# Merging two residue tails per key tile in a dilated attention and soft MoE kernel

The kernel runs on one core of one Trainium2 chip. The metric is the device time of one launch in microseconds (us). The profile of one execution gives its span, which is about 1.7 us shorter than that time. An execution that is clearly longer than the fastest of the same kernel (by over 1.5%) is called slow, and only fast ones are compared.

## The reference

Attention over 8 batches of 8 heads, 576 positions, head size 64. Four heads see the last 32 positions. The other four see every fourth of the last 128, so each of their positions meets only keys of its own residue modulo 4. A soft mixture of experts follows on the 4608 rows of 512.

```python
rel = pos[:, None] - pos[None, :]
mask_plain = (rel >= 0) & (rel < 32)
mask_dil = (rel >= 0) & (rel < 128) & (rel % 4 == 0)
scores = np.where(masks, 0.125 * np.matmul(q, k.transpose(0, 1, 3, 2)), -1e9)
x = softmax(scores) @ v                 # (4608, 512) after the heads are joined
logits = x @ phi                        # 32 slots, 4 for each of 8 experts
d = softmax over the 4608 rows of logits
slot_out[e] = relu((d.T @ x)[e] @ w1[e]) @ w2[e]
out = softmax over the 32 slots of logits @ slot_out
```

## The kernel before

A residue has 144 positions (`SUB`): one tile of 128 and a tail of 16 (`LEFT`). The results of the four tails of a head share one block of 128 rows in `xd`, 32 rows for each, of which 16 are wanted. After the change they fill 64 rows (`NLEFT`). A loop over the batches emits, on TensorE, masks and scores, then products with the values, transposes of the results, logits and slot sums.

```python
def emit_scores(b, g):                    # stage g == 1 holds the tails
    ...
        for r in range(DIL):
            w = LEFT if r < 3 else 2 * LEFT
            jobs.append((kd, SUB * r + 96, qd, SUB * r + 128, W1 + LEFT * r, w))
    ...
    for h in range(4):                    # the mask comes in as a product with ident
        nc.tensor.matmul(sps[h // 2][:, h % 2, 0:n], ident, bias[g], start=True, ...)
    for jn, (kt_, k0, qt_, q0, c0, w) in enumerate(jobs):
        for tt in range(2):
            for h in range(4):
                nc.tensor.matmul(..., kt_[32 * h : 32 * h + 32, k0 : k0 + 128, tt],
                                 qt_[32 * h : 32 * h + 32, q0 : q0 + w, tt], ...)

def emit_av(b, kind, i):                  # a chunk of 6 or 7 (tile, head) units
    ...
        elif t < DIL:                     # whole dilated tiles: 128 rows of output
            jobs.append((0, 128, n, pt[:, h % 2, 128 * t : 128 * t + 128], vD[...]))
        else:                             # tails: four products of 32 rows of output
            for r in range(DIL):
                c0 = W1 + LEFT * r
                jobs.append((32 * r, 32, n, pt[0:48, h % 2, c0 : c0 + 32],
                             vL[b % NV][0:48, h, r, 0 : D + 1]))
    jobs += over                          # overhangs of the plain heads, 32 rows of output
    for k, (p0, np_, n, l, rr) in enumerate(jobs):
        nc.tensor.matmul(o[p0 : p0 + np_, n, :], l, rr, ...)

def back_xT_dil(b, c):
    for r in range(DIL + 1):
        nc.tensor.transpose(rg[:, 128 * r : 128 * r + 128],
                            xd_t[b][:, r, 128 * c : 128 * c + 128], ident)

def slot_out(half, experts):              # products of 256 columns
    for e in experts:
        for c in range(8):
            nc.tensor.matmul(so[half][32 * a : 32 * a + 32, :], hTm[...],
                             w2t[e][:, c, NH * half : NH * half + NH], ...)
```

In `emit_av` the second number of a job is the width of the piece of the array's output that one product uses: 128, or 32.

The softmax here doesn't subtract the row's maximum and nothing guards it: scores larger than these inputs give would overflow.

## Time and profile before

| | before |
|---|---|
| median of 6 runs, us | 182.07 (181.59 to 182.62) |
| profiled span, us | 181.0 |
| TensorE (PE) busy, share of the span | 81% |
| one batch of the loop at full clock, us | 13.67 (101.49 to 115.16) |
| first store issued, us | 152.88 |

The batch is measured between the same product of two successive batches, in a stretch where the granted clock was full.

First the slices of the granted TensorE clock (40 equal slices of the span, 9 is 90% or more of full speed):

```profile
PEclk9999995798589789789999999999855699879855
```

Four lines of the timeline (start, length, engine, line, operation, shapes, count). Lengths of successive products overlap and their ends are modelled, so costs are read from start to start:

```profile
103.08 0.47 PE L339 MATMUL o_d<-v,p 128*128 128x65 f16 x18
103.48 0.53 PE L377 MATMUL rp<-ident,xp 128*128 128x128 f16 x5
...
106.45 0.73 PE L389 MATMUL rd<-ident,xd 128*128 128x128 f16 x10
107.02 0.38 PE L271 MATMUL sa<-masks,ident 128*128 128x512 f16 x1
```

The 18 value products of the chunk with the tails take 103.48 - 103.08 = 0.40 us. The last update of the slot sums shows when the loop ends, and the view of waits shows how long the engine that issues the stores stood before the first one:

```profile
136.80 0.32 DVE L458 TENSOR_TENSOR UT<-UT,u 128x160 f32<-128x160 f32 x1 [1.15 <-PE u L452]
```

```profile
POOL out_dram L746 <- DVE oo L743: 5.8, 1, 5.8
```

### The profile page before, as it was taken

The page shows a single profiled execution, that of the slowest core. Times are in us where ns is not written, and L with a number is a line of the kernel's source. Part 1 is how long each engine was busy: PE and PEld are TensorE (multiplying, and loading weights), DVE is VectorE, ACT ScalarE, POOL GpSimd, SP SyncE. Part 2 cuts the span into 40 slices and gives each one's busy share as a digit, 9 for nine tenths or more (in the row PEclk, how much of TensorE's full clock was granted, in tenths as well). Part 3 has the DMA queues.
Part 4 walks back from the last instruction along what each step waited for, and adds up shares of the span by engine and source line. Part 5 has one row for each costly group of instructions (what it writes and reads, how often), then busy time and mean ns, then how long its engine had stood idle before and what let it go on. Part 6 is the DMA issues. An engine that isn't in the chain of part 4 may idle for free.

```text
span 181.0 us, 5591 instructions
## 1 busy us (share of the span) xinstructions
PE 146.4 (81%) x2464; PEld 87.4 (48%) x2464; DVE 107.5 (59%) x232; ACT 91.0 (50%) x162; POOL 83.9 (46%) x124
## 2 busy tenths in 40 slices
PE   0467977999999999999999999999987986598000
PEld 0133544746755665664674674675735363233000
DVE  4689874875757676588498498453604023389030
ACT  2044454748465484755766776675430024488030
POOL 7953552642623263352544327434410442979900
PEclk9999995798589789789999999999855699879855
DMA  4999999999999999999999999999999999999996
GB/s 60 199 196 208 208 210 214 201 211 214 202 212 214 203 212 214 201 211 213 203 214 211 204 216 210 214 215 215 211 216 213 200 193 163 311 332 409 410 404 239
DMA packets 29527, 40.75 MB, mean 225 GB/s; under 512 B 1856, under 2 KB 19264, under 8 KB 29504
## 3 DMA queue, kind: packets, MB, share of 16 engines
q0 software_dynamic: 28960, 39.36, 116.3%
q1 hardware_dynamic: 544, 1.05, 1.5%
q8 instruction: 19, 0.31, 0.6%
q14 instruction: 4, 0.03, 0.0%
HBM read 61.93 MB, written 9.44 MB: 394 GB/s over the span
## 4 chain that ended last, share of the span: by engine, by line
DMA 43%; PE 34%; ACT 6%; DVE 6%; POOL 5%; issue 3%; POOLq 0%; DVEq 0%
DMA w<-in_moe_w_dram 28%; DMA raw<-in_k_dram 9%; ACT p L293 5%; PE lg L408 5%; PE o_p L339 4%; PE sa L282 4%; DMA out_dram<-ol 4%; PE sb L271 4%; PE sa L271 4%; DMA out_dram<-ot 2%; PE rd L389 2%; DVE qk L245 2%; PE vb L163 2%; PE va L163 2%; PE u L452 2%
## 5 line engine op out<-in xcount | busy, mean ns | idle before, releaser
L293 ACT ACTIVATE p<-sa 128x960 f16<-128x960 f32 (+2 forms) x24 | 21.4, 891 | 33.9 <-PE sb L282 33.4
L339 PEld LDWEIGHTS <-p 128*128 128x128 f16 (+2 forms) x544 | 19.7, 99 | 12.8 <-issue 8.6
L245 DVE STREAM_TRANSPOSE qk<-raw 128x320 uint32<-128x320 uint32 (+1 forms) x32 | 21.6, 678 | 0.3
L271 PE MATMUL sa<-masks,ident 128*128 128x480 f16 (+2 forms) x48 | 15.6, 414 | 7.3 <-POOL masks L489 6.2
L293 ACT ACTIVATE p<-sb 128x960 f16<-128x960 f32 (+2 forms) x24 | 21.2, 884 | 0.0
L236 DVE STREAM_TRANSPOSE qk<-raw 128x576 uint32<-128x576 uint32 x16 | 19.8, 1249 | 0.9 <-DMA raw<-in_q_dram 0.8
L271 PEld LDWEIGHTS <-ident 128*128 128x128 f16 x96 | 9.6, 112 | 18.9 <-issue 7.7
L282 PEld LDWEIGHTS <-qk 32*128 32x128 f16 x832 | 12.6, 100 | 12.0 <-issue 9.8
L408 PE MATMUL lg<-xTd,phi 128*128 128x288 f16 x32 | 18.3, 659 | 0.0
L339 PE MATMUL o_p<-v,p 128*128 128x65 f16 (+1 forms) x288 | 16.6, 202 | 0.8 <-ACT v L172 0.7
L282 PE MATMUL sa<-qk 32*128 32x160 f16 (+4 forms) x416 | 16.5, 217 | 0.8 <-DVE qk L236 0.7
L282 PE MATMUL sb<-qk 32*128 32x160 f16 (+4 forms) x416 | 16.5, 218 | 0.0
L271 PE MATMUL sb<-masks,ident 128*128 128x480 f16 (+2 forms) x48 | 15.4, 411 | 0.5 <-ACT p L293 0.5
L209 POOL COPY v<-v 32x1024 f16<-32x1024 f16 x8 | 8.3, 1036 | 16.1 <-PE sb L282 9.4
L212 POOL DMA_DIRECT2D w<-in_moe_w_dram x16 | 8.9, 554 | 14.4 <-DMA vs<-in_v_dram 6.8
L361 DVE TENSOR_TENSOR xp<-o_p,rc_p 128x448 f16<-128x448 f32 (+1 forms) x24 | 14.4, 602 | 0.8
L361 DVE TENSOR_TENSOR xd<-o_d,rc_d 128x448 f16<-128x448 f32 (+1 forms) x24 | 14.4, 602 | 0.8
L219 POOL DMA_DIRECT2D w<-in_moe_w_dram x10 | 6.7, 673 | 14.5 <-DMA w<-in_moe_w_dram 10.2
L163 PE MATMUL va<-vs,orders 32*128 32x256 f16 (+1 forms) x96 | 12.1, 289 | 1.0 <-ACT p L293 1.0
L412 ACT ACTIVATE ET<-lg 128x288 f16<-128x288 f32 x16 | 6.6, 411 | 12.3 <-PE lg L408 12.1
L360 DVE RECIPROCAL rc_p<-o_p 128x7 f32<-128x7 f32 (+1 forms) x24 | 4.8, 198 | 12.1 <-PE o_p L339 11.6
L382 ACT COPY xTp<-rp 128x576 f16<-128x576 f16 x16 | 10.4, 647 | 2.2 <-PE rp L377 2.2
(108 smaller groups left out, 277.9 us busy)
## 6 DMA issues: line engine op xcount, KB each, us to landing
w<-in_moe_w_dram POOLq DMA_DIRECT2D x16, 512.0 KB, 16.8
w<-in_moe_w_dram POOLq DMA_DIRECT2D x5, 1024.0 KB, 19.3
vs<-in_v_dram POOLq DMA_DIRECT2D x8, 512.0 KB, 14.5
raw<-in_q_dram POOLq DMA_DIRECT2D x7, 576.0 KB, 16.6
raw<-in_k_dram POOLq DMA_DIRECT2D x7, 576.0 KB, 16.8
out_dram<-ot POOLq DMA_DIRECT2D x14, 256.0 KB, 4.2
out_dram<-of POOLq DMA_DIRECT2D x7, 512.0 KB, 4.9
w<-in_moe_w_dram POOLq DMA_DIRECT2D x8, 256.0 KB, 10.2
```

Of the source, the lines that this page charges most:

```text
L163: nc.tensor.matmul(o.rearrange("p (h d) -> p h d", h=4), l, st[:, 0:4, D * r : D * r + D], start=(r == 0), stop=(r == DIL - 1), skip_group ...
L209: nc.gpsimd.tensor_copy(out=vL[b % NV][0:32, :, :, 0:D], in_=vD[b % NV][96:128, :, :, 0:D])
L212: nc.gpsimd.dma_start(out=w1t[e][:, 2 * i : 2 * i + 2, :].rearrange("p l f -> p (l f)"), in_=moe_w1[e, 256 * i : 256 * i + 256].rearrange( ...
L236: nc.vector.transpose(out=dst, in_=src)
L245: nc.vector.transpose(out=o, in_=i)
L271: nc.tensor.matmul(sps[h // 2][:, h % 2, 0:n], ident, bias[g], start=True, stop=False, skip_group_check=True,)
L282: nc.tensor.matmul(sps[h // 2][:, h % 2, c0 : c0 + w], kt_[32 * h : 32 * h + 32, k0 : k0 + 128, tt], qt_[32 * h : 32 * h + 32, q0 : q0 + w ...
L293: nc.scalar.activation(out=pt, in_=sps[ab][:, :, 0:n], func=AF.Exp, scale=SCALE)
L339: nc.tensor.matmul(o[p0 : p0 + np_, n, :], l, rr, start=(k == 0), stop=(k == len(jobs) - 1), skip_group_check=True,)
L361: nc.vector.tensor_tensor(out=x.rearrange("p t (h d) -> p (t h) d", h=4)[0:nq, u0:u1, :], in0=o[0:nq, 0:n, 0:D], in1=rc[0:nq, 0:n, None].b ...
L382: nc.scalar.copy(out=xTp_t[b][:, c, :], in_=rg)
L408: nc.tensor.matmul(lp, phi4[:, kc].rearrange("p c s -> p (c s)"), rhs, start=(kc == 0), stop=(kc == 3))
```

## The change

Its intent is fewer and larger operations. Two residues share one key tile: the keys of the first in rows 0 to 47, a gap, those of the second in rows 64 to 111. Each such tile is multiplied with the tail queries of all four residues, and a mask removes what does not belong. For each head two value products take the place of four: the first writes 128 rows of output, the second the 64 rows that hold the tails. The tails of `xd` are then transposed from 64 rows alone, without zeros. Sums over the slots' exponentials come from the activation that computes them (`accum_out`) instead of products with ones. The outputs of the first six experts are made in products of 512 columns and added later. The core of the diff:

```diff
 emit_scores, stage 1
-                for r in range(DIL):
-                    w = LEFT if r < 3 else 2 * LEFT
-                    jobs.append((kd, SUB * r + 96, qd, SUB * r + 128, W1 + LEFT * r, w))
+                for u in range(2):
+                    jobs.append((kL[b % 2], 128 * u, None, 0, W1 + NLEFT * u, NLEFT))
...
+                    if qt_ is None:
+                        qq = qd[heads, 0:S, tt].rearrange("p (r i) -> p i r", r=DIL)[:, 128:SUB]
 emit_av
-                for r in range(DIL):
-                    c0 = W1 + LEFT * r
-                    jobs.append((32 * r, 32, n, pt[0:48, h % 2, c0 : c0 + 32], vL[...][0:48, h, r, ...]))
+                for u in range(2):
+                    c1 = W1 + NLEFT * (u + 1)
+                    m = (128, 64)[u]
+                    jobs.append((128 - m, m, n, pt[:, h % 2, c1 - m : c1], vL[b % NV][:, h, u, 0 : D + 1]))
 back_xT_dil
         for r in range(DIL + 1):
+            p0 = 0 if r < DIL else NLEFT
             nc.tensor.transpose(
-                rg[:, 128 * r : 128 * r + 128], xd_t[b][:, r, 128 * c : 128 * c + 128], ident
+                rg[:, 128 * r : 128 * r + 128 - p0],
+                xd_t[b][p0:128, r, 128 * c : 128 * c + 128],
+                ident[p0:128, p0:128],
             )
 back_logits
-        nc.scalar.activation(out=ET[:, c0 : c0 + n], in_=lp, func=AF.Exp, scale=1.0)
+        nc.scalar.activation(out=ET[:, c0 : c0 + n], in_=lp, func=AF.Exp, scale=1.0,
+                             accum_out=esum[:, 2 * b + half : 2 * b + half + 1])
 back_u
-            jobs.append((4, ones[0:n, :], er[0:n, t, :]))
 end
-        slot_out(0, ORDER[:6])
-        slot_out(1, ORDER[:6])
-        slot_out(0, HALVED)
+        slot_out(so_early, 0, early, True, True)     # 512 columns
+        nc.scalar.copy(out=early_sb, in_=so_early)
+        for n in range(2):
+            slot_late(0, n)                          # ends with so_sb = early_sb + so
```

Cut here: the gather of the tail keys into `kL`, the copies of the tail values in the new order, the masks with their selects, the mask on the slot weights, which is no longer needed, and the slot weights' transposes, where one product of 128 rows takes the place of four.

More of the change, by code (lines that the diff above doesn't have):

```diff
@@ L37 @@
 LEFT = SUB - 128
-NLEFT = 5 * LEFT
+NLEFT = DIL * LEFT
 WQ = 128 + WINDOW
@@ L63 @@
     consts = ctx.enter_context(tc.tile_pool(name="consts", bufs=1))
-    masks = consts.tile([128, W1 + NLEFT], FP16, name="masks")
-    halves = consts.tile([128, 1], FP32, name="halves")
+    masks = consts.tile([128, W1 + 2 * NLEFT], FP16, name="masks")
     turn = consts.tile([128, 32], FP16, name="turn")
@@ L68 @@
         masks[:, None, 0:WQ].broadcast_to([128, 3, WQ]),
-        masks[:, 0 : W1 + NLEFT],
+        masks[:, 0 : W1 + 2 * NLEFT],
         masks[:, None, 0:128].broadcast_to([128, DIL, 128]),
@@ L76 @@
     ones = consts.tile([128, 128], FP16, name="ones")
-    emask = consts.tile([128, NE, N_SLOTS], FP16, name="emask")
+    esum = consts.tile([128, 2 * B], FP32, name="esum")
+    gap = consts.tile([128, 1], FP32, name="gap")
+    etot = consts.tile([N_SLOTS, 1], FP32, name="etot")
+    ediag = consts.tile([N_SLOTS, N_SLOTS], FP32, name="ediag")
+    ones32 = consts.tile([N_SLOTS, 128], FP32, name="ones32")
     ET = consts.tile([128, N_ROWS + 64], FP16, name="ET")
-    UT = consts.tile([128, 5, N_SLOTS], FP32, name="UT")
+    UT = consts.tile([128, 4, N_SLOTS], FP32, name="UT")
     rcol = consts.tile([128, N_SLOTS], FP32, name="rcol")
@@ L93 @@
     QK_SLAB, V_SLAB = 2 * (S + 64 + S + 80 + S + S + 16), 4096
-    kTp, kTd, qTp, qTd, vP, vD, vL = [], [], [], [], [], [], []
+    kTp, kTd, qTp, qTd, vP, vD, vL, kL = [], [], [], [], [], [], [], []
     for i in range(2):
@@ L104 @@
         vP.append(slab[:, 0:n].rearrange("p (m h d) -> p m h d", m=NT, h=4))
-        for dst in (vD, vL):
-            dst.append(slab[:, n : n + 16 * VW].rearrange("p (h r d) -> p h r d", h=4, r=DIL))
-            n += 16 * VW
+        for dst, r in ((vD, DIL), (vL, 2)):
+            dst.append(slab[:, n : n + 4 * r * VW].rearrange("p (h r d) -> p h r d", h=4, r=r))
+            n += 4 * r * VW
+        kL.append(slab[:, n : n + 512].rearrange("p (s t) -> p s t", t=2))
     def slab_weights(e, tag, n):
@@ L204, in spread_v @@
         )
-        nc.gpsimd.tensor_copy(
-            out=vL[b % NV][32 : 32 + LEFT, :, :, 0:D],
-            in_=sb[0:LEFT, 4:8].rearrange("a h (r d) -> a h r d", r=DIL),
-        )
-        nc.gpsimd.tensor_copy(out=vL[b % NV][0:32, :, :, 0:D], in_=vD[b % NV][96:128, :, :, 0:D])
+        low = sb[0:LEFT, 4:8].rearrange("a h (u w d) -> a h u w d", u=2, w=2)
+        for w in range(2):
+            nc.gpsimd.tensor_copy(
+                out=vL[b % NV][64 * w + 32 : 64 * w + 32 + LEFT, :, :, 0:D], in_=low[:, :, :, w, :]
+            )
+        high = vD[b % NV][96:128].rearrange("p h (u w) d -> p h u w d", w=2)
+        for w in range(2):
+            nc.gpsimd.tensor_copy(
+                out=vL[b % NV][64 * w : 64 * w + 32, :, :, 0:D], in_=high[:, :, :, w, 0:D]
+            )
     def load_w1(e, i):
@@ L248, with gather_left @@
     ptile = {}
+    def gather_left(b):
+        dst = kL[b % 2].rearrange("p s t -> p (s t)").bitcast(U32).rearrange("p (r i) -> p r i", r=DIL)
+        src = kTd[b % 2][:, 0:S].rearrange("p s t -> p (s t)").bitcast(U32)
+        nc.vector.tensor_copy(
+            out=dst[:, :, 0 : LEFT + 32], in_=src.rearrange("p (r i) -> p r i", r=DIL)[:, :, 96:SUB]
+        )
     def emit_scores(b, g):
@@ L258, in emit_scores @@
             if g == 1:
-                for r in range(DIL):
-                    w = LEFT if r < 3 else 2 * LEFT
-                    jobs.append((kd, SUB * r + 96, qd, SUB * r + 128, W1 + LEFT * r, w))
-                n = W1 + NLEFT
+                for u in range(2):
+                    jobs.append((kL[b % 2], 128 * u, None, 0, W1 + NLEFT * u, NLEFT))
+                n = W1 + 2 * NLEFT
         else:
@@ L281, in emit_scores @@
                 for h in range(4):
+                    heads = slice(32 * h, 32 * h + 32)
+                    if qt_ is None:
+                        qq = qd[heads, 0:S, tt].rearrange("p (r i) -> p i r", r=DIL)[:, 128:SUB]
+                    else:
+                        qq = qt_[heads, q0 : q0 + w, tt]
                     nc.tensor.matmul(
                         sps[h // 2][:, h % 2, c0 : c0 + w],
-                        kt_[32 * h : 32 * h + 32, k0 : k0 + 128, tt],
-                        qt_[32 * h : 32 * h + 32, q0 : q0 + w, tt],
+                        kt_[heads, k0 : k0 + 128, tt],
+                        qq,
                         start=False,
@@ L325, in emit_av @@
                 pt = ptile[(b, 1, h // 2)]
-                for r in range(DIL):
-                    c0 = W1 + LEFT * r
-                    jobs.append(
-                        (
-                            32 * r,
-                            32,
-                            n,
-                            pt[0:48, h % 2, c0 : c0 + 32],
-                            vL[b % NV][0:48, h, r, 0 : D + 1],
-                        )
-                    )
+                for u in range(2):
+                    c1 = W1 + NLEFT * (u + 1)
+                    m = (128, 64)[u]
+                    jobs.append((128 - m, m, n, pt[:, h % 2, c1 - m : c1], vL[b % NV][:, h, u, 0 : D + 1]))
         jobs += over
@@ L386, in back_xT_dil @@
             xTd_t[b] = xT_pool.tile([128, 2, DIL, SUB], FP16, name=f"xTd_{b}", tag="xTd")
-        rg = ring.tile([128, 640], FP16, name=f"rd_{b}_{c}", tag="ring")
+        rg = ring.tile([128, S], FP16, name=f"rd_{b}_{c}", tag="ring")
         for r in range(DIL + 1):
+            p0 = 0 if r < DIL else NLEFT
             nc.tensor.transpose(
-                rg[:, 128 * r : 128 * r + 128], xd_t[b][:, r, 128 * c : 128 * c + 128], ident
+                rg[:, 128 * r : 128 * r + 128 - p0],
+                xd_t[b][p0:128, r, 128 * c : 128 * c + 128],
+                ident[p0:128, p0:128],
             )
@@ L396, in back_xT_dil @@
             out=xTd_t[b][:, c, :, 128:SUB],
-            in_=rg[:, 512:640].rearrange("p (r i) -> p r i", r=DIL)[:, :, 0:LEFT],
+            in_=rg[:, 512:S].rearrange("p (i r) -> p r i", r=DIL),
         )
@@ L411, in back_logits @@
         c0 = b * S + n * half
-        nc.scalar.activation(out=ET[:, c0 : c0 + n], in_=lp, func=AF.Exp, scale=1.0)
+        nc.scalar.activation(
+            out=ET[:, c0 : c0 + n],
+            in_=lp,
+            func=AF.Exp,
+            scale=1.0,
+            accum_out=esum[:, 2 * b + half : 2 * b + half + 1],
+        )
     def back_erow(b):
@@ L426, in back_erow @@
             )
-        for r in range(DIL):
-            nc.tensor.transpose(
-                ep[32 * r : 32 * r + 32, NT + DIL, :],
-                ET[0:32, b0 + 512 : b0 + 640].rearrange("p (i r) -> p r i", r=DIL)[:, r, :],
-                ident[0:32, 0:32],
-            )
+        nc.tensor.transpose(
+            ep[:, NT + DIL, :],
+            ET[0:32, b0 + S - 128 : b0 + S],
+            ident[0:32, 0:32],
+        )
         er = s_pool.tile([128, NE, N_SLOTS], FP16, name=f"er_{b}", tag="er")
         er_t[b] = er
-        nc.vector.tensor_tensor(out=er, in0=ep, in1=emask, op=ALU.mult)
+        nc.vector.tensor_copy(out=er, in_=ep)
     def back_u(b):
-        up = ring.tile([128, 5, N_SLOTS], FP32, name=f"u_{b}", tag="ring")
+        up = ring.tile([128, 4, N_SLOTS], FP32, name=f"u_{b}", tag="ring")
         er = er_t.pop(b)
@@ L441, in back_u @@
         for t in range(NT):
-            n = 128 if t < 4 else TAIL
             for c in range(2):
-                x = xp_t[b][0:n, t, :].rearrange("p (x l) -> p l x", l=2)
-                jobs.append((c, x[:, c, :], er[0:n, t, :]))
-            jobs.append((4, ones[0:n, :], er[0:n, t, :]))
+                x = xp_t[b][:, t, :].rearrange("p (x l) -> p l x", l=2)
+                jobs.append((c, x[:, c, :], er[:, t, :]))
         for r in range(DIL + 1):
+            p0 = 0 if r < DIL else NLEFT
             for c in range(2):
-                x = xd_t[b][:, r, :].rearrange("p (x l) -> p l x", l=2)
-                jobs.append((2 + c, x[:, c, :], er[:, NT + r, :]))
+                x = xd_t[b][p0:128, r, :].rearrange("p (x l) -> p l x", l=2)
+                jobs.append((2 + c, x[:, c, :], er[p0:128, NT + r, :]))
         for i, (c, l, rr) in enumerate(jobs):
@@ L465, in prologue @@
         load_qk(1, 0, (0,))
-        nc.vector.memset(masks, 0.0)
+        nc.vector.memset(masks[:, 0:W1], 0.0)
+        nc.vector.memset(masks[:, W1:], MASKED)
+        for u in range(2):
+            own = masks[:, W1 + NLEFT * u : W1 + NLEFT * u + NLEFT].rearrange("p (i r) -> p i r", r=DIL)
+            nc.vector.memset(own[:, :, 2 * u : 2 * u + 2], 0.0)
+        nc.vector.memset(gap, 0.0)
         nc.vector.memset(ones, 1.0)
@@ L475, in prologue @@
             nc.vector.memset(vD[i][:, :, :, D : D + 1], 1.0)
-            nc.vector.memset(vL[i][:, :, :, D : D + 1], 1.0)
+            nc.vector.memset(kL[i], 0.0)
+            nc.vector.memset(vL[i], 0.0)
+            for p0 in (0, 64):
+                nc.vector.memset(vL[i][p0 : p0 + 32 + LEFT, :, :, D : D + 1], 1.0)
         load_qk(0, 0, (1,))
@@ L479, in prologue @@
         load_v(0)
-        left = masks[:, W1:].rearrange("p (u c) -> p u c", c=LEFT)
+        left = [
+            masks[:, c0 : c0 + NLEFT].rearrange("p (i r) -> p r i", r=DIL)[:, 2 * u : 2 * u + 2]
+            for u, c0 in enumerate((W1, W1 + NLEFT))
+        ]
         band = (
@@ L484, in prologue @@
             (masks[:, 0:WQ], masks[:, 0:WQ], [[-1, WQ]], WINDOW - 1, 1, ALU.is_ge, MASKED),
-            (left, left, [[0, 5], [1, LEFT]], 32, -1, ALU.is_ge, MASKED),
-            (left, left, [[0, 5], [-1, LEFT]], -1, 1, ALU.is_ge, MASKED),
-        )
+            (gap, gap, [[0, 1]], -48, 1, ALU.is_ge, MASKED),
+            (gap, gap, [[0, 1]], 63, -1, ALU.is_ge, MASKED),
+        )
+        for x in left:
+            band += (
+                (x, x, [[64, 2], [1, LEFT]], 32, -1, ALU.is_ge, MASKED),
+                (x, x, [[-64, 2], [-1, LEFT]], -1, 1, ALU.is_ge, MASKED),
+            )
         for dst, src, pattern, base, mult, op, fill in band:
@@ L513, in prologue @@
         nc.vector.tensor_copy(out=masks[:, WQ:W1], in_=masks[:, 0:TAIL])
+        nc.vector.tensor_scalar(
+            out=masks[:, W1:], in0=masks[:, W1:], scalar1=gap, scalar2=None, op0=ALU.max
+        )
         qk_plain(0, 0)
         qk_plain(1, 0)
-        nc.vector.memset(emask, 1.0)
+        nc.vector.memset(ones32, 1.0)
         for i in range(1, 4):
@@ L568, in slot0 @@
             qk_dil(1, b, 1)
+            gather_left(b)
             emit_scores(b, 0)
@@ L576, in slot0 @@
             nc.vector.memset(siTm, 0.0)
-            nc.vector.tensor_reduce(
-                out=halves, in_=orders[:, 0, 0:TAIL], axis=mybir.AxisListType.X, op=ALU.add
-            )
-            nc.vector.tensor_copy(
-                out=emask[:, NE - 1, :], in_=halves.broadcast_to([128, N_SLOTS])
-            )
         if b1:
@@ L665 @@
         nc.vector.memset(hTm[g], 0.0)
-    nc.vector.reciprocal(out=rcol, in_=UT[:, 4, :])
+    nc.vector.tensor_reduce(out=etot, in_=esum[0:N_SLOTS], axis=mybir.AxisListType.X, op=ALU.add)
+    nc.vector.tensor_scalar(
+        out=ediag, in0=ident[0:N_SLOTS, 0:N_SLOTS], scalar1=etot, scalar2=None, op0=ALU.mult
+    )
+    total = ring.tile([128, N_SLOTS], FP32, name="total", tag="ring")
+    nc.tensor.matmul(total, ones32, ediag, start=True, stop=True)
+    nc.vector.reciprocal(out=rcol, in_=total)
     diag = bass.AP(
@@ L714, with slot_out, slot_late @@
     psum_e.release()
+    so_early = ring.tile([128, DMODEL], FP32, name="so_early", tag="ring")
+    early_sb = fix.tile([128, QK_SLAB], FP16, name="early_sb", tag="qk1")
+    early_sb = early_sb[:, 0 : 2 * DMODEL].bitcast(FP32)
     so = [psum_so.tile([128, NH], FP32, name=f"so{i}", tag=f"so{i}") for i in range(2)]
-    def slot_out(half, experts):
-        for e in experts:
-            for c in range(8):
-                g, j, a = e // 4, e % 4, c % 4
-                nc.tensor.matmul(
-                    so[half][32 * a : 32 * a + 32, :],
-                    hTm[2 * g + c // 4][:, c % 4, 32 * j : 32 * j + 32],
-                    w2t[e][:, c, NH * half : NH * half + NH],
-                    start=(e == ORDER[0] and c < 4),
-                    stop=(e == ORDER[-1] and c >= 4),
-                )
-        if experts[-1] == ORDER[-1]:
-            nc.scalar.copy(out=so_sb[:, NH * half : NH * half + NH], in_=so[half])
+    def slot_out(dst, c0, parts, first=False, last=False):
+        n = dst.shape[1]
+        jobs = [(e, c) for e, chunks in parts for c in chunks]
+        for i, (e, c) in enumerate(jobs):
+            g, j, a = e // 4, e % 4, c % 4
+            nc.tensor.matmul(
+                dst[32 * a : 32 * a + 32, :],
+                hTm[2 * g + c // 4][:, c % 4, 32 * j : 32 * j + 32],
+                w2t[e][:, c, c0 : c0 + n],
+                start=first and i < 4,
+                stop=last and i >= len(jobs) - 4,
+            )
+    def slot_late(half, n):
+        slot_out(so[half], NH * half, late[n : n + 1], n == 0, n == len(late) - 1)
+        if n == len(late) - 1:
+            cols = slice(NH * half, NH * half + NH)
+            nc.vector.tensor_tensor(out=so_sb[:, cols], in0=early_sb[:, cols], in1=so[half], op=ALU.add)
     psum_f = tc.alloc_tile_pool(name="psum_f", bufs=4, space=bass.MemoryType.PSUM)
@@ L818 @@
     with tc.manual_schedule(engines=None):
-        slot_out(0, ORDER[:6])
-        slot_out(1, ORDER[:6])
-        slot_out(0, HALVED)
+        early = [(e, range(8)) for e in ORDER[:6]]
+        late = [(e, range(8)) for e in HALVED]
+        slot_out(so_early, 0, early, True, True)
+        nc.scalar.copy(out=early_sb, in_=so_early)
+        for n in range(2):
+            slot_late(0, n)
         at = {5: 0}
@@ L825 @@
             if pair in at:
-                slot_out(1, (HALVED[at[pair]],))
-        slot_out(1, HALVED[1:])
+                slot_late(1, at[pair])
+        slot_late(1, 1)
         for pair in range(NSPLIT // 2, NFIN // 2 - 2):
```

## The prediction

> **What bounds the kernel now.** I read the page's slices first, then its account of HBM, then the chain of work that ended last, then the table by stretches over the last 43 us, then the groups.
>
> The slices and the account of HBM:
>
> ```profile
> DMA  4999999999999999999999999999999999999996
> GB/s 60 199 196 208 208 210 214 201 211 214 202 212 214 203 212 214 201 211 213 203 214 211 204 216 210 214 215 215 211 216 213 200 193 163 311 332 409 410 404 239
> HBM read 61.93 MB, written 9.44 MB: 394 GB/s over the span
> raw<-in_k_dram POOLq DMA_DIRECT2D x7, 576.0 KB, 16.8
> ```
>
> The DMA engines are full from the second slice to the last but one. The rate counts bytes as written: loads turn fp32 into fp16, so the plateau near 210 GB/s is 420 GB/s read, and the 410 GB/s at the end is stores. The loads write 61.93 / 2 = 30.97 MB, at 0.21 MB/us 147.5 us. The stores take 9.44 / 0.41 = 23.0 us. Together 170.5 us of 181 are data movement, which the change leaves byte for byte. The last line says that a load lands 16.8 us after its issue. At 0.21 MB/us that is 3.5 MB ahead of it, about six loads. This queue is why a late issue in the middle does no harm.
>
> The chain, in order of time, shows the same from the other side:
>
> ```profile
> 85.86 0.29 issue
> 86.15 16.32 DMA raw<-in_k_dram
> 102.47 0.30 issue
> ...
> 146.34 10.34 DMA w<-in_moe_w_dram
> 156.68 0.04 issue
> 156.72 0.32 PE so L722 x4
> 157.04 0.02 issue
> 157.06 0.38 ACT so_sb L730
> 157.44 0.04 issue
> 157.48 2.73 PE f L801 x6
> ```
>
> Before 86 us the chain runs through compute, after it through transfers until the last weights land at 156.68. I do not read the first part as "compute sets the end": the load issued at 86.15 had 16 us of others before it, so an earlier issue would have lengthened its wait. From 156.68 on stand the steps that a change can lengthen: last slot products, copy of so_sb, first full-width output products.
>
> The table by stretches finds where the DMA engines are not full (columns: stretch, its length, busy time of PE, PEld, DVE, ACT, POOL, granted clock, DMA share, GB/s):
>
> ```profile
> 138.00:143.00 5.00, 4.13 (x40) 1.57 (x44) 0.82 (x5) 0.38 (x1) 2.21 (x3) 0.50 1.12 209
> 143.00:150.00 7.00, 6.12 (x144) 3.88 (x137) 1.33 (x4) 1.13 (x3) 2.21 (x3) 0.98 1.42 195
> 152.00:154.00 2.00, 1.79 (x20) 1.00 (x18) 1.71 (x4) 1.82 (x5) 1.12 (x3) 1.00 0.83 116
> 157.00:160.00 3.00, 2.53 (x10) 0.89 (x8) 1.36 (x2) 1.94 (x4) 2.15 (x4) 0.50 1.86 375
> 160.00:161.00 1.00, 1.00 (x5) 0.49 (x4) 0.89 (x2) 0.88 (x3) 0.86 (x2) 0.80 0.70 136
> 161.00:179.00 18.00, 6.01 (x27) 2.39 (x25) 7.63 (x11) 7.13 (x15) 10.42 (x15) 0.77 1.56 406
> 179.00:181.00 2.00, 0.00 (x0) 0.00 (x0) 0.00 (x0) 0.00 (x0) 0.00 (x0) 0.50 0.08 29
> ```
>
> Three holes: 152 to 154 (loads ebb, stores have not begun) loses 2 x (195 - 116) / 195 = 0.8 us; 160 to 161 (half-width stores done, the first full-width one waits for so_sb) loses (406 - 136) / 406 = 0.7 us; the last 2 us wait for the final store. Filling both middle holes would give 1.5 us, 0.8%, still inside "same".
>
> How much slack has compute ahead of 152? In the timeline the slot products wait for weights:
>
> ```profile
> 151.04 0.29 PE L722 MATMUL so<-w,hTm 128*32 128x256 f16 x4 [1.11 <-DMA w<-in_moe_w_dram]
> ```
>
> So compute may become 1.1 us later before the first store moves. That store can then move by another 0.8 us before the full-width stores do, because POOL stood idle that long before issuing them.
>
> **What the Trainium skill says.** "DMA: Bandwidth & Descriptors", section Bandwidth, puts the ceiling of the ports into SBUF at 435 GB/s and a 16 MB load at 425; the 420 (read) and 410 (stores) here agree, so nothing is left to gain in rate. "Perfetto Trace Analysis", section Identifying the Most-Contended Engine, says that a busy matmul row is no measure of how near TensorE is to its limit, and to look at weight loads and at HBM: here PE is 81% busy, PEld 48%, and HBM 394 GB/s. "TensorE: Matmul & The Clock Gate", section What's actually happening, has the clock halve after an idle window of about 3.4 us and return after a busy one; the table agrees, 0.50 at 138 to 143 and at 157 to 160. "VectorE: DVE Perf Modes", section Why PSUM operands drop a tier, allows fp32 from PSUM one element per cycle; the 128x448 product from PSUM took 624 ns and the 128x384 one 557, about 1.05 ns per element over 155 ns of fixed time, which agrees.
>
> **The change part by part.**
>
> Tails, scores. Per batch 32 products of 16 or 32 columns become 16 of 64, and the mask products of that stage widen from 304 to 352 columns. The old 32 issue within 0.23 us of the timeline (78.25 to 78.48). The new ones read queries with a jump between neighbouring columns. The logits show what that costs: the four lg products of one half take 1.33 us; two read contiguously (2 x 0.12 us at the 0.42 ns per column of the mask products), leaving about 0.54 us each for the two that jump, 1.9 ns per column. Sixteen products, four heads at once, 64 x 1.9 = 0.12 us: 0.48 us, so +0.25. Wider masks: 4 x 48 x 0.42 ns = +0.08.
>
> Tails, values and the rest on PE. Eight fewer value products (18 took 0.40 us): -0.18. Three fewer of 13 transposes of the slot weights (0.55 us): -0.13. Five fewer of 25 products in u (1.0 us): -0.2. PE in sum: about -0.2 us per batch.
>
> ACT. The exponential of that stage goes from 608 to 704 elements, at 0.83 ns each (608 took 677 ns, 960 took 971) +0.08 us, twice per batch. The sums written beside ET add perhaps 0.1 us twice. DVE: a gather of 128x192 words, about 0.35 us, from the 128x160 copy of 325 ns. POOL: the same elements in half-sized copies, about the same time. In all a batch changes by -0.2 to +0.3 us, over eight by -2 to +2.5 us, none of it on the transfers.
>
> Prologue. Four more selects on POOL at 0.28 us, which DVE now waits for before its first transposes: +1.2 us for the first batch. The next batches' loads then pace it, so I count nothing.
>
> Slot outputs. 96 products of 256 columns at about 31 ns each (3.0 us) become 48 of 512 at a quarter of 0.215 us (2.6 us): -0.4 us, spent before the wait for weights. The copy of early_sb, 128x512 from PSUM, is 0.69 us and lies in that wait. What touches the path: so_sb is now a DVE sum, 155 + 256 x 1.05 = 0.42 us, in place of the 0.37 us ACT copy: +0.05 us before the first store and +0.05 us after the last weights.
>
> Sum on the path: 0 in the load stream, +0.05 to +0.1 us at the end. 182.08 becomes about 182.1 us.
>
> **The rivals.** (1) Compute set the pace up to 86 us, so a lighter TensorE starts loads earlier and gains. For: PE busy 81%, and loads wait for DVE's transposes to free their buffer, 1.9 us at the longest. Against: not one slice between has DMA below 9 tenths. If it held, -0.2 us x 8 gives 180.5. (2) The jumping reads of four heads do not run side by side: 16 x 0.12 = 1.9 us in place of 0.23, net +1.3 us per batch, +10 over eight. After the 1.9 us of slack the end moves by some 8: 190. Against: the old products visibly overlap by heads. A milder form, compute 3 us late, gives about 183. (3) PE finishes early, idles, and its clock is half when the first stores are computed: +0.3 us before the first store. That shortens the hole at 160 by as much, so nothing: 182.1. (4) Earlier slot sums pull stores into the hole at 152: 181.3. Against: the timeline shows the weights, not PE, ending that wait.
>
> **Range and chances.** The centre is the sum. Half the first rival or all of the fourth sets the low end, 181.3; the milder second one the high end, 183.1. Past 2% (178.4 or 185.7) only the second rival in full gets: faster 0.02, same 0.94, slower 0.04.
>
> **What would show it right or wrong.** Right: the DMA slices keep their plateau, the last weights land at 156.7 within 0.5 us, the holes stay, the so_sb sum takes 0.42 us, and the wait of the slot products for weights remains. Each size has its own test: PE busy falls by about 2 us in the loop, u falls from 25 products to 20, the tail products issue within 0.5 us, the early slot products take 2.6 us. Wrong: a load plateau above 210 GB/s or an earlier last weight (rival 1); the slot products not waiting for weights at all (rival 2); a first store issued well before 152.9 us (rival 4).

## The result

| | before | after |
|---|---|---|
| median of 6 runs, us | 182.07 (181.59 to 182.62) | 195.97 (194.09 to 199.39) |
| profiled span, us | 181.0 | 192.4 |
| one batch at full clock, us | 13.67 | 15.04 (44.91 to 59.95) |
| last slot sums, us | 136.80 | 150.54 |
| first store issued, us | 152.88 | 164.43 |

The ratio of fast runs is 1.072 (95%: 1.065 to 1.079): the changed kernel is slower. A ratio here is the mean time of one kernel's fast runs over that of the other's in the same rounds, so not quite the ratio of the medians quoted beside it. Two of the six runs after, 198.26 and 199.39 us, were slow and are left out of it.

Now the same views of the changed kernel. The slices first, with the rate of the DMA engines:

```profile
PEclk9999995799999699999789957985975589998855
...
GB/s 70 191 201 205 210 210 219 200 209 210 209 209 206 213 209 204 211 214 204 209 217 200 216 213 215 213 213 170 210 205 196 196 23 0 171 375 411 409 379 223
```

The load plateau is at 210 GB/s as before, and then the DMA engines stop: 23, 0 and 171 GB/s in slices 33 to 35. In the kernel before no slice after the first is below 163. The table by stretches (stretch, length, busy time of PE, PEld, DVE, ACT, POOL, clock, DMA share, GB/s) narrows it down:

```profile
155.00:157.00 2.00, 2.00 (x36) 0.89 (x32) 0.42 (x1) 0.39 (x1) 0.00 (x0) 0.83 0.05 11
157.00:164.00 7.00, 5.52 (x94) 2.87 (x87) 1.62 (x5) 2.06 (x5) 0.00 (x0) 1.00 0.00 0
164.00:166.00 2.00, 1.86 (x20) 0.91 (x17) 2.00 (x4) 1.78 (x6) 1.57 (x3) 1.00 0.33 69
```

For 7 us nothing is transferred. All weights are there (the last landed at 155.57 us, 1.1 us earlier than before), PE works, and no store can be issued yet:

```profile
POOL out_dram L794 <- DVE oo L791: 17.7, 1, 17.7
```

The wait for the first store grew from 5.8 to 17.7 us. The first store is 164.43 - 152.88 = 11.55 us later, and the span is 192.4 - 181.0 = 11.4 us longer: one for one. And the delay was there when the loop ended:

```profile
150.54 0.29 DVE L478 TENSOR_TENSOR UT<-UT,u 128x128 f32<-128x128 f32 x1 [0.90 <-PE u L472]
```

That is 13.7 us later than before, of which about 2.3 us were slack. So the loop must be explained. The timeline of one batch, same groups as before:

```profile
46.67 1.26 PE L352 MATMUL o_d<-v,p 128*128 128x65 f16 x10
47.87 0.53 PE L390 MATMUL rp<-ident,xp 128*128 128x128 f16 x5
...
51.00 0.99 PE L403 MATMUL rd<-ident,xd 128*128 128x128 f16 x10
51.92 0.60 PE L286 MATMUL sa<-masks,ident 128*128 128x512 f16 x2
```

Ten value products take 47.87 - 46.67 = 1.20 us where 18 took 0.40. Ten transposes take 0.92 us where the same number took 0.57. The batch, group by group from start to start of the two timelines:

| group of one batch | before, us | after, us | difference |
|---|---|---|---|
| dilated value products of the last chunk | 0.40 | 1.20 | +0.80 |
| transposes `rd` | 0.57 | 0.92 | +0.35 |
| scores of the tails | 0.34 | 0.54 | +0.20 |
| masks of that stage | 0.61 | 0.71 | +0.10 |
| wait for ACT before `vb` | 0.50 | 0.67 | +0.17 |
| transposes of slot weights `ep` | 0.49 | 0.39 | -0.10 |
| slot sums `u` | 0.84 | 0.69 | -0.15 |
| sum | | | +1.37 |

The sum is the whole growth of the batch, 15.04 - 13.67. Times eight it is 11.0 us. The rest has to do with the clock. The slot sums are updated once per batch (the `UT` lines), and the times between the first six updates show what half clock costs: 16.06, 15.25, 14.33, 13.67 and 13.67 us before, 15.03, 15.97, 15.07, 15.87 and 17.55 us after. Above the undisturbed 13.67 and 15.03 that is 4.6 us before and 4.3 us after. In these five the kernel before was at half clock for 12.7 us and the kernel after for 13.9, so half clock cost about a third of its length, and the mean clock from 40 to 120 us is the same in both, 0.91. The kernel after then has one stretch more in the loop, 6.8 us from 128.4; a third of it is 2.3 us. Both loops also end at half clock, the last 7.1 us before and the last 8.5 us after. 11.0 + 2.3 = 13.3 us is an estimate, and 13.7 was measured.

### The profile page after: what moved, and what is told of

It is laid out like the page before. It is cut to its first block, busy times and chain, and to the rows that moved or that the text cites. A ratio compares the mean times of both kernels' runs of the same rounds, so it can differ in the third digit from the quotient of the medians.

```text
span 192.4 us, 5048 instructions
## 1 busy us (share of the span) xinstructions
PE 156.8 (82%) x2162; PEld 89.9 (47%) x2162; DVE 111.9 (58%) x253; ACT 93.9 (49%) x177; POOL 87.4 (45%) x144
## 5 line engine op out<-in xcount | busy, mean ns | idle before, releaser
L352 PEld LDWEIGHTS <-p 128*128 128x128 f16 (+1 forms) x480 | 24.6, 102 | 16.2 <-issue 10.2
L216 POOL COPY v<-v 32x512 f16<-32x512 f16 x16 | 9.8, 611 | 30.7 <-DVE v L206 30.3
L286 PE MATMUL sa<-masks,ident 128*128 128x480 f16 (+2 forms) x48 | 16.4, 432 | 7.3 <-POOL masks L525 6.2
L313 ACT ACTIVATE p<-sb 128x960 f16<-128x960 f32 (+2 forms) x24 | 21.9, 911 | 0.0
L302 PEld LDWEIGHTS <-qk 32*128 32x128 f16 x576 | 11.0, 105 | 14.5 <-issue 11.0
L302 PE MATMUL sa<-qk 32*128 32x160 f16 (+2 forms) x288 | 15.3, 247 | 2.2 <-DVE qk L245 2.2
L286 PE MATMUL sb<-masks,ident 128*128 128x480 f16 (+2 forms) x48 | 16.7, 439 | 0.4 <-ACT p L313 0.3
L352 PE MATMUL o_d<-v,p 128*128 128x65 f16 x192 | 16.5, 202 | 0.0
L302 PE MATMUL sb<-qk 32*128 32x160 f16 (+2 forms) x288 | 15.3, 247 | 0.0
L221 POOL DMA_DIRECT2D w<-in_moe_w_dram x16 | 8.9, 555 | 6.5 <-DMA vs<-in_v_dram 2.8
```

The costliest lines, as they stand in the source:

```text
L216: nc.gpsimd.tensor_copy(out=vL[b % NV][64 * w : 64 * w + 32, :, :, 0:D], in_=high[:, :, :, w, 0:D])
L221: nc.gpsimd.dma_start(out=w1t[e][:, 2 * i : 2 * i + 2, :].rearrange("p l f -> p (l f)"), in_=moe_w1[e, 256 * i : 256 * i + 256].rearrange( ...
L302: nc.tensor.matmul(sps[h // 2][:, h % 2, c0 : c0 + w], kt_[heads, k0 : k0 + 128, tt], qq, start=False, stop=(jn == len(jobs) - 1 and tt == 1),
L313: nc.scalar.activation(out=pt, in_=sps[ab][:, :, 0:n], func=AF.Exp, scale=SCALE)
L352: nc.tensor.matmul(o[p0 : p0 + np_, n, :], l, rr, start=(k == 0), stop=(k == len(jobs) - 1), skip_group_check=True,)
```

## The experiments

The diffs below are cut to the lines that matter.

**The theory** came from where the dear products lie. In the last chunk the order is 128, 128, then four times 128 and 64 rows of output. The ten `rd` transposes change between 128 and 64 rows of input in the same manner. The Trainium skill, "TensorEngine Tiling (Array Packing)", section Key Properties, says: "Mode switching requires drain: Changing tiling mode (not just tile) drains the TensorE". It gives no duration. Up to the 128-wide transposes that follow there are eight changes. At 0.029 us between products without a change, (1.20 - 10 x 0.029) / 8 = 0.11 us for each (the expectations below say 0.12, and call a change a switch). **Rivals:** the 64-wide products are slow in themselves (their operands come from a new layout), or the chunk waits for the new value tiles, or the longer ACT work.

### Both tail products 128 wide

```diff
-                    m = (128, 64)[u]
-                    jobs.append((128 - m, m, n, pt[:, h % 2, c1 - m : c1], vL[...][:, h, u, 0 : D + 1]))
+                    jobs.append((0, 128, n, pt[:, h % 2, c1 - 128 : c1], vL[...][:, h, u, 0 : D + 1]))
```

The product is larger: it reads columns of the other half too. What they give lands in rows 0 to 63 of the tails' block, which no later step uses.

> The changed kernel with both tail value products of a head 128 output rows wide (the upper one was 64), results the same. Theory (switching the array between a 128-column and a 64-column shape costs about 0.12 us each time, eight times per batch): the last ten products of o_d fall from 1.2 us to about 0.3 us at full clock, 0.9 us per batch, about 7 us over eight batches, all of it seen at the end: 188 us. Rival (a tail value product costs 0.12 us by itself, because of its operands): the ten stay at 1.2 us and the time at 195. Rival (DVE gather or POOL copies pace the loop): the ten fall, the time does not.

Measured: 181.8 us (181.7 to 182.99, 4 runs), ratio 0.9997 (0.9960 to 1.0033) to the kernel before. The timeline and the last slot sums:

```profile
45.23 0.48 PE L351 MATMUL o_d<-v,p 128*128 128x65 f16 x10
45.54 0.52 PE L389 MATMUL rp<-ident,xp 128*128 128x128 f16 x5
...
134.79 0.29 DVE L477 TENSOR_TENSOR UT<-UT,u 128x128 f32<-128x128 f32 x1 [0.89 <-PE u L471]
```

The ten products fall from 1.20 to 0.31 us. More work in each of four of them made the chunk four times as fast, and the whole loss is gone: 14 us from one line. That is more than the switches alone give: 8 x (15.04 - 14.11) = 7.4 us of 15.75 by which the loop ends earlier, and the run is 6 us faster than the 188 us expected. The other 8 us show in the clock. The five times between updates of the slot sums, 15.03 to 17.55 us in the changed kernel, are 14.08 to 14.10 us here, and the sixth falls from 15.09 to 11.21 us:

```profile
PEclk9999999699999999999999999999985897899655
```

No slice from 36 to 130 us is below 9 tenths any more; the changed kernel has six such slices there, and the kernel before seven.

### The same products in another order

```diff
-                    jobs.append((128 - m, m, n, pt[...], vL[...]))
+                    (jobs, over)[u].append((128 - m, m, n, pt[...], vL[...]))
```

All 128-wide products come first, then the four 64-wide ones: the work of the changed kernel to the last product, with two changes of shape in place of eight.

> The changed kernel with the same ten products, 128 and 64 wide as they were, but all 128-wide ones first, then the four 64-wide ones. Theory (the switch costs, not the width): two switches in place of eight, the ten take about 0.5 us, 0.7 us less per batch, 190 us. Rival (the 64-wide product itself is slow): four slow products remain, about 0.5 us or more above the wide version, and start-to-start of about 130 ns among the 64-wide ones.

Measured: 183.41 us (182.11, 182.13, 184.69 and one slow run of 185.05), ratio of fast runs 1.007 (0.998 to 1.016).

```profile
45.21 0.60 PE L354 MATMUL o_d<-v,p 128*128 128x65 f16 x10
45.74 0.53 PE L392 MATMUL rp<-ident,xp 128*128 128x128 f16 x5
```

The chunk takes 0.53 us, as the theory said; the time of the run, expected at 190 us, fell further, as in the run before. This rules out the 64-wide product itself and its operands, and any wait for the tiles. It is **the change of shape**. Against the wide version two changes cost (0.53 - 0.31) / 2 = 0.11 us each, and the eight of the changed kernel (1.20 - 0.31) / 8 = 0.11 us. In the records of this run the steps are 0.123 us into the 64-wide group and 0.127 out of it, against 0.03 to 0.05 between its members. Whether the products themselves or the loads of their weights wait at a change, no run here parts.

### Transposes of all 128 rows

```diff
-            p0 = 0 if r < DIL else NLEFT
-                rg[:, 128 * r : 128 * r + 128 - p0], xd_t[b][p0:128, r, ...], ident[p0:128, p0:128]
+                rg[:, 128 * r : 128 * r + 128], xd_t[b][:, r, 128 * c : 128 * c + 128], ident
```

The value products keep alternating.

> The changed kernel with the tail transposes taking all 128 rows again, as in the kernel before. Theory (a transpose of 64 rows among ones of 128 is a switch as well): the ten rd transposes fall from 0.92 to 0.52 us, 0.4 us per batch, 3 us over eight: 192 us. Rival (no switch cost for rows): nothing, 195 us.

Measured: 192.37, 192.0 and two slow runs of 197.56 and 197.92 us; ratio of fast runs 1.055 (1.052 to 1.059). So the transposes are the smaller part. Its batch is 14.66 us at full clock, and its mean granted clock between 40 and 120 us, 0.87, is the lowest of all kernels:

```profile
PEclk9999997599579759969987999996998599997855
...
148.56 0.29 DVE L475 TENSOR_TENSOR UT<-UT,u 128x128 f32<-128x128 f32 x1 [0.90 <-PE u L469]
```

### Both together

> Both edits. Theory: about 10.6 us of the 11.5 us by which compute was late is gone, and the rest lies within the 1.9 us of slack ahead of the stores: 182 to 183.5 us, equal to the kernel before, and the slot products wait for weights again. Rival (other parts of the change carry a few us too: jumping reads, DVE gather, sums, the longer chain after attention): 185 to 187 us.

Measured: 182.07 us (181.88 to 182.24), ratio 0.9996 (0.9975 to 1.0017).

```profile
48.56 0.73 PE L401 MATMUL rd<-ident,xd 128*128 128x128 f16 x10
49.13 0.59 PE L286 MATMUL sa<-masks,ident 128*128 128x512 f16 x2
```

The transposes are back at 0.57 us, so the 64-row tails cost 0.35 us per batch, about 0.1 us for each of the four changes. The batch takes 13.78 us, 0.11 more than in the kernel before. No microsecond of the end comes from it: with both shapes mended the change is neutral, as with the first mended alone.

### Lateness without changes of shape

The theory has a second part, that the changes of shape also cost clock. To part the direct cost from the clock, this kernel makes TensorE late by dense work: on the one above, the mask products of the 512-wide stage are issued twice. The second overwrites the first, and the result is the same.

```diff
-        for h in range(4):
+        for h in tuple(range(4)) * (2 if g == 2 else 1):
```

> The version without the switches (both edits) with the four mask products of the 512-wide score stage issued twice: 4 x 0.215 = 0.86 us more of dense work on TensorE per batch, and no more switches. A batch at full clock then takes 13.78 + 0.86 = 14.6 us, as long as in the changed kernel with only its transposes mended (14.6 us, 192 to 198 us in all). Theory (switches also [...]halves the clock in several windows of the loop, which is the other half of the loss): no half-clock window between 40 and 120 us here, compute 6.9 us later against 2.8 us of wait for weights, 183 to 185 us. Rival (only the lateness at full clock counts, whatever fills it): the same as the version with mended transposes, 190 us or more.

Measured: 183.05 us (182.06 to 184.29), ratio 1.0059 (1.0010 to 1.0107).

```profile
PEclk9999999699999999999999999999998599999755
...
138.95 0.29 DVE L474 TENSOR_TENSOR UT<-UT,u 128x128 f32<-128x128 f32 x1 [0.89 <-PE u L468]
```

The batch is 14.64 us at full clock, as long as that of the kernel with alternating value products alone, yet the loop ends 9.6 us sooner and the clock stays full. In the table by stretches, over the same 80 us of the loop, that kernel and then this one:

```profile
40.00:120.00 80.00, 78.30 (x1190) 48.06 (x1189) 54.29 (x116) 48.17 (x91) 33.14 (x53) 0.87 1.13 203
```

```profile
40.00:120.00 80.00, 77.97 (x1317) 47.42 (x1313) 57.98 (x126) 51.51 (x99) 35.20 (x56) 1.00 1.15 210
```

PE counts as busy for 98% and 97% of it in both, and the granted clock is 0.87 against 1.00. So the lost clock is a **second cost** and no result of being late. That changes of shape bring it is not shown: the kernel before has 0.91 in the same 80 us. The run shows the slack too: the loop ends 2.15 us later than in the kernel before, and the profiled span (180.3 us) is no longer for it. Two of the four runs were 1.8 and 2.2 us longer, which suggests that it is about used up.

### Changes of shape put into the kernel before

The opposite test: nothing of the change, only an order. In the last third of the plain value products the overhangs of 32 rows of output are interleaved with the products of 128 instead of following them, which gives ten more changes of shape per batch.

```diff
-        jobs += over
+        if kind == "p" and i == 2:
+            jobs = [j for pair in zip(jobs, over) for j in pair]
+        else:
+            jobs += over
```

> The kernel before, unchanged but for the order of products in the last third of the plain values: its six 32-wide overlap products stand between the six 128-wide ones, not after them. Same instructions, same operands, ten more switches per batch. Theory: 10 x 0.12 = 1.2 us per batch, about the changed kernel's own burden (8 + 4 more switches), so about its time, 190 to 197 us, with half-clock windows in the loop. Rival (the switches are not the cause; the changed operands are): 182 us.

Measured: 190.4 us (189.76 to 191.49), ratio 1.047 (1.043 to 1.051). The same instructions in another order make the kernel before 8 us slower.

```profile
117.96 1.69 PE L342 MATMUL o_p<-v,p 128*128 128x65 f16 x12
119.58 0.42 PE L411 MATMUL lg<-xTp,phi 128*128 128x288 f16 x2
...
147.59 0.32 DVE L461 TENSOR_TENSOR UT<-UT,u 128x160 f32<-128x160 f32 x1 [1.14 <-PE u L455]
```

The twelve products take 119.58 - 117.96 = 1.62 us where the kernel before takes 0.58 (110.41 to 110.99): 1.04 us for ten changes, 0.10 us each, here between 128 and 32 columns. A batch at full clock grows by the same, from 13.67 to 14.71 us. In eight batches that makes 8.3 of the 10.8 us by which the loop ends later. The mean clock between 40 and 120 us was 0.91, that of the kernel before. The other 2.5 us fall together with more half clock from 120 us to the end of the loop, 12 us against 7; this part was not tested.

### The rest of the change alone

The kernel before with the slot sums from ACT and the 512-wide early slot outputs, and nothing of the tails:

```diff
+            accum_out=esum[:, 2 * b + half : 2 * b + half + 1],
-            jobs.append((4, ones[0:n, :], er[0:n, t, :]))
-        slot_out(0, ORDER[:6]); slot_out(1, ORDER[:6]); slot_out(0, HALVED)
+        slot_out(so_early, 0, early, True, True); nc.scalar.copy(out=early_sb, in_=so_early)
+        for n in range(2): slot_late(0, n)
```

> The kernel before with the two other parts of the change alone (slot sums from ACT; early slot products 512 wide with their copy and the DVE sum), its tails as they were. Theory (they are neutral, as predicted): 181.5 to 182.5 us, five fewer products in u, and the so_sb sum 0.42 us. Rival (the longer chain after attention or the accumulating exponentials cost): 183 us or more.

Measured: 181.95 us (181.47 to 182.37), ratio 0.9994 (0.9971 to 1.0017). Neutral, as predicted for these parts. Its loop ends at 136.82 us, as before (136.80), although its mean granted clock over the span is low: 0.854 to 0.868 in these four runs, 0.837 to 0.861 in the six of the changed kernel. Here a low clock alone did not make the end late.

### Can a freed end be used? Two tries

With both shapes mended, the loop ends 2.5 us earlier than before, and the time is the same. Stores are at the end, so I looked for a hole among them. There was one, at 174 to 176 us (table by stretches):

```profile
174.00:176.00 2.00, 0.00 (x0) 0.00 (x0) 1.45 (x2) 1.28 (x2) 0.00 (x0) 0.50 0.91 208
```

The last two output tiles wait there for buffers whose stores have not landed. The first try gives these two tiles the space of weights no longer needed:

```diff
-            tag = "last0" if pair == NFIN // 2 - 2 else "last1"
-            ot = out_pool.tile([128, 2, DMODEL], FP32, name=f"ol_{pair}", tag=tag)
+                ot = w1t[pair - (NFIN // 2 - 2)][:, 0:2, :].rearrange("p l f -> p (l f)")
+                ot = ot.bitcast(FP32).rearrange("p (k n) -> p k n", k=2)
```

> The version without the switches, and the last two output tiles in the space of first-layer weights that are no longer needed, not in the two buffers of earlier output tiles. In that version the stores run dry from 174 to 176 us (281 and 136 GB/s in place of 408) because the last two tiles wait for a store to land before they are written. Theory: this hole closes, 1.0 to 1.3 us: 180.8 to 181.2 us, under both kernels. Rival (the stores are the bound in any order): 182.0 us.

Measured: 184.54 us (184.36 to 185.52, 5 runs), ratio 1.015 (1.013 to 1.018), longer rather than shorter.

```profile
174.00:178.00 4.00, 0.00 (x0) 0.00 (x0) 0.00 (x0) 0.00 (x0) 0.00 (x0) 0.50 1.67 391
178.00:179.00 1.00, 0.00 (x0) 0.00 (x0) 0.00 (x0) 0.00 (x0) 0.00 (x0) 0.50 1.10 216
179.00:181.00 2.00, 0.00 (x0) 0.00 (x0) 0.00 (x0) 0.00 (x0) 0.00 (x0) 0.50 0.10 19
181.00:183.80 2.80, 0.00 (x0) 0.00 (x0) 0.00 (x0) 0.00 (x0) 0.00 (x0) 0.50 0.00 0
```

The hole is filled. In the profiled run, the longest of the five, the last store landed at 180.82 us, and the program ended at 183.8, 3.0 us later. Here the stores that POOL issues land last. In the kernel it builds on, those that SP issues land last, at 179.60 us, with the end 0.9 us after. Why the end takes longer I did not settle.

The second try keeps the order of landings and only exchanges buffers, so that the last two tiles reuse those of earlier stores:

```diff
-            tag = "last0" if pair == NFIN // 2 - 2 else "last1"
+            tag = "last1" if pair == NFIN // 2 - 1 else "last0"
-            if pair == NFIN // 2 - 3:
+            if pair == NFIN // 2 - 4:
```

> The version without the switches (both edits), with the two last output tiles (still written late, still stored by the SP queue) in the buffers of two earlier stores: those of pair 14 and of the fifth half-width pair, which land at about 173.2 and 173.8 us, in place of those that land at 173.8 and 175.1. Theory: the last two tiles are written 0.7 and 1.3 us earlier, the hole of 281 and 136 GB/s from 174 to 176 us closes for the greater part, and the SP stores remain the last to land, so that the end follows them by about 1 us as it does now: 181.0 to 181.6 us. Rival (as in the version with own buffers, the end is held up by something after the last store that SP does not issue): 182 us or more.

Measured: 181.95 us (181.66 to 182.66, 6 runs), ratio 0.9997 (0.9975 to 1.0018). No gain, though the hole is closed:

```profile
174.00:176.00 2.00, 0.00 (x0) 0.00 (x0) 0.71 (x2) 0.60 (x1) 0.00 (x0) 0.50 1.65 399
```

The last landings stayed where they were (178.35 and 179.61 us, against 178.34 and 179.60). In both kernels the landings keep one cadence, about 0.66 us per 256 KB. A low packet rate in one stretch was no gap in what landed. My theory of the hole fell in both tries. None of the nine kernels beats the kernel before; four equal it within 0.1%.

## Why the prediction was wrong

**The step that failed** is the one on the values: "Eight fewer value products (18 took 0.40 us): -0.18." It priced products by their number. The ten take 1.20 us, +0.80 in place of -0.18. The two experiments on their width and order show why: what costs is the change between 128 and 64 rows of output, 0.11 us, and the diff's `m = (128, 64)[u]` inside the loop over heads makes eight of them.

**A cost that the sum left out:** the tails' transposes from 64 rows. Only their neighbour was counted. They cost +0.35 us per batch, measured by giving them back their 128 rows. A sign stood in the timeline of the kernel before: its five transposes `rp`, one of which has 64 rows, take 103.94 - 103.48 = 0.46 us, and the ten of `rd`, all of 128 rows, 0.57, or 0.28 for five.

**The batch in sum:** "-0.2 to +0.3 us" was +1.37. Without these two terms it would have been +0.22, inside the interval. Other terms held: tail scores +0.20 (predicted +0.25), wider masks +0.10 (+0.08), slot weights -0.10 (-0.13), `u` -0.15 (-0.2), gather 0.26 us (0.35), so_sb sum 0.42 us (0.42), early slot products about 2.5 us (2.6). Two were off and did not matter for the result: the activation's sum is an instruction of its own of 0.194 us, and POOL's copies take 2.44 us instead of 2.07 per batch.

**What no term covered** is the clock. I read half clock in the kernel before as what follows idleness, and took 0.50 at 138 to 143 us for agreement with the skill's page on the clock gate. That reading was wrong. This stretch begins at 129.7 us, and in the ten microseconds before it PE is busy for 85% or more of each; earlier in the loop half clock comes with PE busy throughout, in both kernels. The clock is worth about 8 us of the 15.75 between the changed kernel and the one with wide products. Between kernels that carry the change it goes with the alternating value products: of the seven tried, the one that kept them has a mean clock of 0.87 between 40 and 120 us, five have 1.00 and one 0.98. Wide products do not keep it away for good: with both shapes mended half clock begins at 124 us, ten us before the loop ends. And the kernel before (0.91) and the one with the rest of the change alone (0.90) have such stretches without those products, at no loss for their end. So what exactly trips it stays open.

One more reading was loose: the prediction holds 420 GB/s of reads against a ceiling for the ports into SBUF, but what entered SBUF was 210. Nothing in the sum rests on it, and the plateau stayed.

**The rivals.** The second had the scenario right: compute late beyond "the 1.9 us of slack", the slot products no longer waiting for weights, an end near 190. Its mechanism was wrong. The jumping reads of the four heads do run side by side, 0.11 us for four of 64 columns. I gave it 0.04 because I judged that mechanism, when the scenario could be reached by any term of the loop. The first rival, compute as the bound up to 86 us, did not come: the loop ended 3.3 us earlier in the second try on the stores (133.5 us against 136.8), and the time did not fall. The slack itself was sized well: the loop 13.7 us later and the end 11.4 leaves 2.3.

## What to carry to other kernels

Before merging small products, write down for each product in issue order how many rows and columns of the array it uses, and count the changes: here each cost 0.10 to 0.11 us, nearly as much as four products of 65 columns, and with the smaller products widened to the shape of their neighbours the chunk took a quarter of the time. If two shapes are needed, group them. And when the end is bound by transfers, judge a rival by whether compute could use up the slack by any means, not by the first mechanism that comes to mind.

## What the Trainium skill lacked or had wrong

- "TensorEngine Tiling (Array Packing)", section Key Properties, names the drain at a change of mode but not its size. Here, at full clock: 0.11 us between 128 and 64 columns of output (eight changes, 1.20 us for ten products; two changes, 0.53 us; none, 0.31 us), 0.10 us between 128 and 32 columns, about 0.1 us between 128 and 64 rows of input. That the array drains is the page's word; the runs show only the time. It applies also between the full array and a half of it, which is what a "tail" makes without looking like packing.
- "TensorE: Matmul & The Clock Gate", section What's actually happening, ties half clock to an idle window. Here the mean granted clock from 40 to 120 us is 0.91 in both kernels, where PE counts as busy for 78.31 (after) and 78.64 (before) of 80 us; with the tail products made wide it is 1.00, at 77.98 of 80. A busy PE row does not show that the clock will stay. PE's ends are modelled, so short idle times within that row may not show, and no run here tells whether they were the cause.
- "SBUF — State Buffer", section Door 1: The DMA port swizzle, says that each access to a new 16-byte line pays a penalty, without a figure. The tail scores, whose neighbouring query columns lie far apart, took 0.11 us per 64 columns with four heads side by side, 1.7 ns per column, against 0.42 ns for contiguous reads.
- "ScalarE: Activation LUTs" names the accumulator output of an activation but not that reading it is an instruction of its own: 194 ns after each of the 16 activations.
- No page that I read has this: the program ended 3.0 us after the last landing where POOL's stores landed last, and 0.9 us after it where SP's did.
